# Score bursts at alternating ends of three PSUM banks, and weights through six buffers, in a fused attention and SwiGLU kernel

## The chip, the cores and the metric

The kernel runs on one core of a Trainium2 chip. The metric is the device time of one execution in microseconds (us); a lower time is better. The time before is 532.54 us, the median of three runs (531.28 to 533.48).

## What is computed

Eight batches of eight heads attend over 576 tokens with a head dimension of 64. A score survives only if it is within `tau` (0.02) of the largest of its row; the softmax runs over the survivors. The 4608 rows of 512 that come out are normalised and go through a SwiGLU layer with an inner width of 1536.

```python
scores = scale * np.matmul(q, k.transpose(0, 1, 3, 2))
thresh = np.max(scores, axis=-1, keepdims=True) - tau
scores = np.where(scores >= thresh, scores, -1000000000.0)
scores = scores - np.max(scores, axis=-1, keepdims=True)
attn = np.exp(scores)
attn = attn / (np.sum(attn, axis=-1, keepdims=True) + 1e-09)
attn_out = np.matmul(attn, v)
...
x = attn_out.transpose(0, 2, 1, 3).reshape(B * S, H * D)
xn = x / np.sqrt(np.mean(x * x, axis=-1, keepdims=True) + 1e-06) * rms_g
g = xn @ w_gate
return (g / (1.0 + np.exp(-g)) * (xn @ w_val)) @ w_out
```

## The kernel before

**Steps.** The work is cut into 144 steps. A step is one chunk of 128 query rows (`chunks`, L281) with one pair of heads; four steps make a chunk, and 36 chunks cover all rows. The first 16 steps belong to batch 0, and batch 1 begins at step 16. For each step:

- TensorE multiplies the queries with the keys of both heads (`emit_burst`, letter S) into PSUM, 576 columns per head. The matmuls are float32, on 64 rows each.
- VectorE reduces each head (`ttr`, letter r): it copies the scaled scores to SBUF (tile `ssb`) and takes the largest (tile `mx`, or `mxp` for a piece that is not the last of its head). When it has read a PSUM bank, that bank is free again.
- GpSimd (POOL) adds `tau` to get the threshold (`nthr`, letter n, tile `nth`).
- ScalarE masks each head (`prelu`, letter p, two per step) and takes the exponential of both (`ex2`, letter x, tile `wsb`).
- The weights are transposed: for the first 16 steps on TensorE, in two PSUM banks (letter T), with two copies by VectorE (letter S on VectorE, tile `wt`); later by a DMA transpose that SP issues (letter t).
- TensorE multiplies them with the values for two steps at a time (`emit_av`, letter A), and VectorE divides by the sum (letter h, tile `xsb`).

After the fourth step of a chunk the rows are squared on ScalarE (letter S there, tile `xn`), normalised on POOL (m, N) and transposed. A group of two or four chunks then goes through the feed-forward layer (`emit_ffn`, L1048): twelve gate products (G) and twelve value products (V) on TensorE, tanh on ScalarE (t), two products on VectorE (s, g; tiles `sl` and `hf`), and the output products (O).

**Bursts.** `plan_bursts` (L787) cuts the scores into TensorE bursts as the constant `CHOP` (L1302) says: kind "w" for steps 0 to 8, bursts of 1024 columns for steps 8 to 24, and bursts of 1536 columns from there on. A "w" burst is one step: each head is cut in two halves of 288 columns on the two sides of a bank border, so it fills parts of banks 0 and 1 for head 0, and 3 and 4 for head 1, the same for each step. A burst of 1024 or 1536 columns takes up to two or three banks per head and begins and ends inside a step where it has to; a step that is cut needs two reductions per head in place of one. PSUM has eight banks. Transposes and the other products take single banks, whose numbers follow the letter in the order: `T67` uses banks 6 and 7.

**Order.** `ORDER` (L43) lists the instructions of each engine, one letter for each unit of work as `LETTERS` (L26) names them. A letter takes the oldest unit of its kind that is left; `.k` after it skips k of them. `in_order` (L128) turns this into queues. Each engine works through its own queue strictly in this order, and waits where its next unit is not ready; DMAs from SP are issued in SP's order. Costs and due times in the source no longer set the order; the texts do.

**Weights.** The gate and value weights come in twelve loads of 512 KB (L1216, letter i on SP), each into one of three stages of the tile `stg` (L255), in turn. POOL scales and rounds each load in two casts (letter c; tiles `wg` and `wv`). A load waits for the casts of the load that had the stage before. The last stage also holds the first query rows at the start (L447). The 24 buffers `hf` for the hidden values are twelve of their own and twelve that lie on the stages (L257, L258); the first gate into one of the latter waits for all casts (L1100). Output weights are four loads that POOL issues (letter M).

The batch loads are D, d, m, M (batch 0's queries and keys), L and o (batch 1's queries, keys and tails), O and A (values), l and a (later batches). TensorE transposes batch 1's queries and keys in four units (letter q) and tails (k, l).

Of the kernel before, what the change touches and what calls it, by code (L numbers as in the profile page):

```python
# [10 lines left out]
FP16 = mybir.dt.float16  # L11
# [1382 lines left out]
```

## Time and profile before

| what | value |
|---|---|
| median of three runs | 532.54 us (531.28 to 533.48) |
| profiled execution, its own time | 533.18 us |
| its span, first to last instruction | 531.4 us |
| TensorE (PE) busy | 508.1 us, 96% |
| VectorE (DVE) busy | 459.5 us, 86% |
| ScalarE (ACT) busy | 443.9 us, 84% |
| GpSimd (POOL) busy | 224.0 us, 42% |
| granted TensorE clock | 0.999 |
| prelu (`ssb<-ssb,nth`) | 288 of 766 ns |
| exponential (`wsb<-ssb`) | 144 of 1157 ns |
| weight loads (`stg<-in_moe_w_gate_dram`, `stg<-in_moe_w_val_dram`) | 12 of 512 KB, 4.9 and 5.2 us from issue to landing |

The profile is of one execution. Nearly all instructions carry the line number of one helper (L99), so a group is known by its tiles: `bank<-qkt` is a score matmul, `bank<-id,wsb` a weight transpose, `bank<-xnT,wg` a gate product, `ssb<-bank,zcol` a reduction. A busy TensorE is not TensorE at its peak, because matmuls are pipelined and their ends are modelled. Waits name the engine and tile that came last before the wait ended. "SPq" is SP's queue of DMA issues.

### The profile page before, as it was taken

How to read it: one execution, taken by the hardware profiler on the slowest of the kernel's cores; microseconds unless marked ns; L12 is line 12 of the kernel's file. 1: busy time of each engine (PE TensorE's matmuls, PEld its weight loads, DVE VectorE, ACT ScalarE, POOL GpSimd, SP SyncE). 2: the span in 40 equal slices, each digit the busy share in tenths (PEclk: the TensorE clock that was granted, in tenths of full speed). 3: DMA queues.
4: the chain of work that ended last, by engine and by line, in shares of the span. 5: the costliest groups of instructions: out<-in, count | busy, mean ns of one | idle time of the engine just before them, and what ended most of it. 6: DMA issues, size and time to landing. Idle time of an engine off the chain costs nothing.

```text
span 531.4 us, 14442 instructions
## 1 busy us (share of the span) xinstructions
PE 508.1 (96%) x5344; PEld 268.0 (50%) x5344; DVE 459.5 (86%) x1276; ACT 443.9 (84%) x648; POOL 224.0 (42%) x478
## 2 busy tenths in 40 slices
PE   7887889999989999999999999999999999989995
PEld 4555655564545455545455444544545455444442
DVE  4899989998999799999998989998999898864653
ACT  5999989998799899799999889889899889971211
POOL 0464678445742446517553255726751230121000
PEclk9999999999999999999999999999999999999999
DMA  9999899799979999898989998999885686555202
GB/s 198 251 252 214 223 208 197 136 233 204 171 144 156 175 208 174 167 195 154 224 152 174 186 176 158 190 199 213 179 150 107 146 156 113 103 107 110 59 21 80
DMA packets 218887, 88.52 MB, mean 167 GB/s; under 512 B 195264, under 2 KB 204992, under 8 KB 218816
## 3 DMA queue, kind: packets, MB, share of 16 engines
q1 hardware_dynamic: 216016, 85.49, 81.2%
q0 software_dynamic: 1600, 1.57, 1.8%
q8 instruction: 42, 0.69, 0.5%
q10 hardware_dynamic: 1200, 0.52, 0.3%
q14 instruction: 29, 0.24, 0.2%
HBM read 37.75 MB, written 9.44 MB: 89 GB/s over the span
## 4 chain that ended last, share of the span: by engine, by line
PE 66%; DVE 5%; DMA 3%; ACT 2%; issue 2%; POOL 1%; SPq 0%; POOLq 0%; DVEq 0%; ACTq 0%
PE bank L99 66%; DVE ssb L99 3%; DMA wt<-wsb 2%; ACT ssb L99 1%; DVE qkt L99 1%; ACT wsb L99 1%; DMA qkx<-in_k_dram 1%; DVE hf L99 1%; DVE sl L99 1%; ACT th L99 0%; DVE xsb L99 0%; POOL spare L99 0%; POOL qkx L99 0%; DVE stg L99 0%; ACT xn L99 0%
## 5 line engine op out<-in xcount | busy, mean ns | idle before, releaser
L99 ACT ACTIVATE ssb<-ssb,nth 128x576 f32<-128x576 f32 x288 | 209.6, 766 | 14.4 <-POOL nth L99 14.1
L99 DVE CUSTOM_DVE_ANT_0 ssb<-bank,zcol 128x576 f32<-128x576 f32 (+5 forms) x288 | 182.9, 671 | 17.5 <-PE bank L99 12.7
L99 ACT ACTIVATE wsb<-ssb 128x1152 f16<-128x1152 f32 x144 | 165.6, 1157 | 2.1 <-DMA wt<-wsb 0.4
L99 PE MATMUL bank<-qkt 64*64 64x512 f32 (+11 forms) x2232 | 155.6, 410 | 5.4 <-DVE mx L99 3.9
L99 PE MATMUL bank<-xnT,wg 128*128 128x512 f16 (+1 forms) x480 | 113.3, 358 | 2.9 <-DVE mx L99 2.1
L99 PE MATMUL bank<-xnT,wv 128*128 128x512 f16 (+1 forms) x480 | 113.3, 358 | 0.3
L99 POOL TENSOR_SCALAR nth<-mx 128x2 f32<-128x2 f32 x144 | 30.8, 214 | 183.2 <-DVE mx L99 171.3
L99 PEld LDWEIGHTS bank<-qkt 64*64 64x64 f32 (+1 forms) x2232 | 73.3, 134 | 63.5 <-issue 23.6
L99 ACT ACTIVATE th<-bank 128x512 f32<-128x512 f32 (+1 forms) x120 | 64.9, 545 | 48.0 <-PE bank L99 47.3
L99 DVE SCALAR_TENSOR_TENSOR sl<-th,bank 128x512 f32<-128x512 f32 (+1 forms) x120 | 74.1, 626 | 19.3 <-ACT th L99 18.8
L99 PEld LDWEIGHTS <-wg 128*128 128x128 f16 x480 | 43.3, 98 | 56.1 <-DVE mx L99 7.3
L99 PEld LDWEIGHTS <-wv 128*128 128x128 f16 x480 | 44.6, 98 | 47.7 <-DVE mx L99 3.5
L99 PEld LDWEIGHTS <-wt 128*128 128x128 f16 (+1 forms) x1440 | 51.2, 100 | 19.4 <-issue 2.6
L99 PE MATMUL bank<-va,wt 128*128 128x65 f16 (+3 forms) x1440 | 54.9, 196 | 2.3 <-DMA wt<-wsb 1.0
L99 PE MATMUL bank<-wo,stg 128*128 128x512 f16 x216 | 51.3, 379 | 0.0
L99 PE MATMUL bank<-wo,hf 128*128 128x512 f16 x216 | 50.8, 379 | 0.0
L99 DVE STREAM_TRANSPOSE qkt<-qkx 128x128 f32<-128x128 f32 (+2 forms) x72 | 41.0, 586 | 0.4 <-POOL qkx L99 0.4
L99 DVE CUSTOM_DVE_ANT_0 ssb<-bank,zcol,mxp 128x384 f32<-128x384 f32 (+7 forms) x76 | 36.2, 508 | 3.2 <-issue 2.1
L99 DVE TENSOR_TENSOR stg<-bank,sl 128x512 f16<-128x512 f32 (+1 forms) x60 | 36.8, 628 | 2.0 <-PE bank L99 1.2
L99 DVE TENSOR_TENSOR hf<-bank,sl 128x512 f16<-128x512 f32 (+1 forms) x60 | 37.0, 628 | 0.9 <-PE bank L99 0.4
L99 POOL COPY spare<-qkx 32x576 f32<-32x576 f32 x48 | 31.6, 658 | 13.1 <-DMA qkx<-in_k_dram 7.5
L99 DVE TENSOR_TENSOR xsb<-bank,rz 128x256 f32<-128x256 f32 x72 | 30.6, 425 | 5.5 <-POOL xn L99 1.4
(45 smaller groups left out, 373.9 us busy)
## 6 DMA issues: line engine op xcount, KB each, us to landing
vst<-in_v_dram SPq DMA_DIRECT2D x32, 256.0 KB, 4.1
qkx<-in_k_dram SPq DMA_DIRECT2D x24, 288.0 KB, 3.7
qkx<-in_q_dram SPq DMA_DIRECT2D x24, 288.0 KB, 3.6
out_dram<-osb SPq DMA_DIRECT2D x48, 128.0 KB, 2.6
stg<-in_moe_w_gate_dram SPq DMA_DIRECT2D x6, 512.0 KB, 4.9
stg<-in_moe_w_val_dram SPq DMA_DIRECT2D x6, 512.0 KB, 5.2
wt<-wsb SPq DMA_TRANSPOSE x128, 3.7
out_dram<-osb SPq DMA_DIRECT2D x8, 256.0 KB, 4.1
```

The costliest lines, as they stand in the source:

```text
L99: made = got(*args, **kw)
```

## The change

Three things change.

- `CHOP` has a new kind "y" for steps 0 to 24. A burst is one step. Even steps lie at the left end of three banks per head (banks 0 and 1 for head 0, 3 and 4 for head 1: 512 columns, then 64). Odd steps lie at the right end (banks 1 and 2, and 4 and 5: 512 columns in bank 2 or 5 first, then 64 in bank 1 or 4). From step 24 bursts have 1536 columns as before.
- `stg` has six stages. All 24 hidden buffers lie on it: the first twelve on stages 3 to 5, the others on stages 0 to 2. `W_SLOTS` says which stage each load takes. The first use of a hidden buffer waits for the casts out of stages 3 to 5, or 0 to 2.
- The five orders are written anew for their first part, and are the same from some point on. In SP's order, four weight loads now stand ahead of the first load of batch 1 (the first L); before, three L stood ahead of the first weight load and the rest were mixed. The orders of all engines differ with that.

```diff
--- before.py
+++ after.py
@@ -42,40 +42,40 @@
 )
 ORDER = dict(
     PE=(
-        "wt.1:1t0t3t.1:6St6t7t2St6t5t7ST67t2ST62t7Sq25T67ST72A6SA6q72ST65T72ST67A2T65x7Sq67A5T72Sq67T25T72Sk5x6T72A5ST67A2T65ST72A6G5T72SV6G7V2G6A5S",
-        "l67V2G5V6G7A2SV7x6G2V5G7V6A2SG7V0G6V3G1O7V4A6SG6V0G3V1x4A6SO.1:6G0OV3G1A2A7OSV6G7V3G0V1A6G4V2G5V7G6SA6V0G7V3G6V1G4V2G5V7G6SV6O7A0G3OV6SO6A3",
-        "G0OV4A1G7V6A2SG6V0G3V1G4V6A7SG7V6SG7A0V6G3V1A7O6SG7V0G3V1G4V7A2A5SOO7OA5SG6V0G3V1G4V6A7SG6V0G3V1G4V6A7SG6O7V0A3OA6SG7V0A6G3V1O7OSG6V7G0A3V1",
-        "G4O6V7A2SOO7OA2SG6V0G3V1G4A6V7SG6V0G3V1G4V7A6SA6O7G0V3OA2SG6V0G7O6V3OSG6V0A3G1V4A7G2V6SO6A7OO7A2SG6V0G3V1G4A6V2OSG7V0G3V6G1A4V7SO6G0OV3A5A7S",
-        "G6V0O7A3G1OV6SG6A0V3G1V4G6V7SO6OA0O7A6SG6V0G3V1A2G4V6OSG6V0G3V1G4V6A2SO6G0A3OV2A7SG6O7V0G3OV2SG6A0V3G7V1G4A6V7SA7O6OA7SG7V0G3V1G4A6O7OSV7G6",
-        "V0G3V1G4V6A2A7SO6G7OV2SG7A0V3G1V4O7OSA6G7V0G3V6G4V7A2SA7O6OSG6V0G3A1V6G4A7V6SG6A7V0G3V1G4V6O7SOG1A2V6G0V3G2V1G0A6V7G5A6V3G0O2OA6V7O5OO1OO7O",
-        "G3V0G5V4G3O2OV0G6V5G2V3O6G4V5G7OO0134V2G6OV7G2V6OOG7OOV5OG7V5G6V7OOOOOOOOOOOOOOOOO",
+        "wt2t.1:5t7t.2:1St5t6t7St7St.1:5T67t4t3ST67SA6T67St3T67ST67ST67SA2T67ST67A0A6x7Sq67Sx3T67T01q67SA2T67G0Sk6V7SG2T67SV3T67G2Sq67V5G0T67V4A1q67S",
+        "T67SG6SV7G6SV2T67A0SG6V7SG6A7SV7A6l23x5G7SV7G0A6V3G1V6G4O7V6SO.1:6x0A3A4O.1G1SOV0G6V3G7V4G6A.1:7SA7V3G0V4G1V6A2G7SV7G6A0V3G7V4G1V2G5V6G7SO6",
+        "V7G3A7OSA6V0G3V4G6O7OSV6G0A1V3G4V7G5V6SG6V7A5A2SG6A7V0G3A7V4O6SG7V0G3V4G1A2V7A5SO.1:7O.1OA2SG6V0G3V1G4V7A6SG6V0G3V1G4V6A7SG6O7V0A3OA6SG7V0A6",
+        "G3V1O7OSG6V7G0A3V1G4O6V7A2SOO7OA2SG6V0G3V1G4A6V7SG6V0G3V1G4V7A6SA6O7G0V3OA2SG6V0G7O6V3OSG6V0A3G1V4A7G2V6SO6A7OO7A2SG6V0G3V1G4A6V2OSG7V0G3V6",
+        "G1A4V7SO6G0OV3A5A7SG6V0O7A3G1OV6SG6A0V3G1V4G6V7SO6OA0O7A6SG6V0G3V1A2G4V6OSG6V0G3V1G4V6A2SO6G0A3OV2A7SG6O7V0G3OV2SG6A0V3G7V1G4A6V7SA7O6OA7SG7",
+        "V0G3V1G4A6O7OSV7G6V0G3V1G4V6A2A7SO6G7OV2SG7A0V3G1V4O7OSA6G7V0G3V6G4V7A2SA7O6OSG6V0G3A1V6G4A7V6SG6A7V0G3V1G4V6O7SOG1A2V6G0V3G2V1G0A6V7G5A6V3",
+        "G0O2OA6V7O5OO1OO7OG3V0G5V4G3O2OV0G6V5G2V3O6G4V5G7OO0134V2G6OV7G2V6OOG7OOV5OG7V5G6V7OOOOOOOOOOOOOOOOO",
     ),
     ACT=(
-        "lT.1TT.2TT.1TTpTpxTTppxppTxppxpVppxpxpVSppxpxppxVppppxxVSppxEppxpppxpppxxpptpxpSxtpptxppvvxpttpSxptpptpxSxppttxtpppxpxppttpxpxppxtppStxppxpp",
-        "xptpttxStpptxppxSttptptptpxxpptxppxppxpptSxpptxSptptxptpppxxptpxpppxptpxtpppxxSptpxtptppxSpxppxppppxStptxtpppxxpptptxtpxppxSpptxppxpptxpStpp",
-        "pxxpptptxptSxppxppxppppSxtxtpptxppxpptptxtpxppSxpptppxppxtxtpSppxpxppxpttptxpSpxppxpppxpxSttpptxppxptpxtptpxppxptppxSpxppxtpptSxppxpptxtpptx",
-        "SppxpppxppxpxttSpptxppxptpxttppxpSppxtpppxppxxptSptpxpxppxttpptxSppxpppxpxptptxtSppxppxppxttptppxpxpptpxpppxtppStppxSxxppptxtptxSppxppppxpxt",
-        "pptxptpxSpxppttp.2p.2txppx.1xSpptxp.2tpptxpxtSttStttttttttttteses",
+        "lT.1TT.3TTTTTppxTp.1Tpxppxppxp.1pTxp.1pxp.1pxppxSp.1pxSp.1Vpxp.1pxVpptxpEpp.1txpp.1pxtpVpxtp.1pVx.1xp.1tpSxtp.1pp.1pxp.1txptxppp.1vvpxtSxp.1",
+        "pp.1ttxp.2tp.1pxxppSxpptpxSpxppttxtp.1pxppxptptxptpSxp.1pxt.1Stptpttxppxp.1tpppxxppp.1txtpSpxpxptpxp.3tp.2tp.1x.1pxpptxpppxSptxtp.1pp.1xpSx",
+        "p.1ptxp.1ttpxp.1Spxppxp.1ppxSptptxtpxppxpptptxptxppxSpptxppxpptxpStpppxxpptptxptSxppxppxppppSxtxtpptxppxpptptxtpxppSxpptppxppxtxtpSppxpxppxp",
+        "ttptxpSpxppxpppxpxSttpptxppxptpxtptpxppxptppxSpxppxtpptSxppxpptxtpptxSppxpppxppxpxttSpptxppxptpxttppxpSppxtpppxppxxptSptpxpxppxttpptxSppxppp",
+        "xpxptptxtSppxppxppxttptppxpxpptpxpppxtppStppxSxxppptxtptxSppxppppxpxtpptxptpxSpxppttp.2p.2txppx.1xSpptxp.2tpptxpxtSttStttttttttttteses",
     ),
     DVE=(
-        "zCR.1RcRrrrrRRrrSSRrrSSrrVSSrrSShrrVhrrSSSSrrSSrrSxShrrrrrhrSVSrrrSrrrVSSSrrvrrhrrSSxrrSrrSSShrrrrSSrrhSSrsrgrrrrshsgrrgrrrrhssgrrxgsrrghsgr",
-        "rtTrssgrsgrghrtrTrrrrrssggxhrrtrrrru.2rseru.2sghhueurrrgrrrsshgsggstgrrsrrhrrTrrssgTggssgsgrrrrghrrseTtgrrrtrhrseghurshgurrrrrsrgsrrgshtgrrr",
-        "rrrsTuTtgrrrrshgsgrruhrrrrrrsgTrsrsghhgrrrrerrhrrrerssggsrrhgrrrrrrssggTsrhrgrrrrrrshgeututrhrrsgrTsrgrehrrrrrsrhsTgrgstTghrurrrurrrheetrrrs",
-        "rrsggsrhrrrrrrgssggshrrgrrrrrhrsTgheturtrsrrsggrurerTrrrrrtrhrssggshTgTrrrrhrurherrrrusrtsgsggrerrrrhrsrgshsrrgrrrrrrsggtherrhrsghrrstregrrr",
-        "rTrrsgsrhgsrTgrrrrurerhuhttrrrrrsrsgusghguTrrrrrsrTgsrsghrgrrrrerhsrgherrrrsrgrTsgterrrrtrrhssggshrrgrrrrrhruthtrrrerssggTTursreurhrrrgrrrTs",
-        "suggsrhhgrrrrrrsgrrrrsgesghrrerrrrrhrsrsgsrhggrrrrrrherrrsgrsghsrrgrhrrrhrrssggsrrrrr.2r.2grhrsseghsgshsggshggeessegesgessggsgesggssgsggsgsg",
-        "eeE",
+        "zCcRRrRrr.1rRr.1rSRRSr.1rS.1SrhrS.1SrrS.1SrrSSrrSSr.1hS.1rSr.1S.1Shrhxr.1rVrxS.1SSSrVrhrSsSrrgvrsrS.1SrgrS.1SsrVrS.1SgshgVr.1rSSr.1rsrrgsrgr",
+        "hSSr.1rsgrrhsrrghxsrTrrrhgssg.1gr.1rsTt.1tgrrrrr.1rhxu.1r.1hsure.1r.1rrrer.1gssgrgTTsh.1tur.1rr.1rgrhssgrhur.1sgrrrgr.1hrrrs.1stgsgssggr.1r",
+        "r.1r.2grrstThetrrhr.1grsgr.1u.1rsuerTrrr.1rrsggr.1hrTtssggrrr.2r.2rrhhsutgrrr.1hrssggr.1rhur.1rrrr.1rsTrgsrgshhgrrrr.2rre.1herrrrssggsrrhgrr",
+        "rrrrssggTsrhrgrrrrrrshgeututrhrrsgrTsrgrehrrrrrsrhsTgrgstTghrurrrurrrheetrrrsrrsggsrhrrrrrrgssggshrrgrrrrrhrsTgheturtrsrrsggrurerTrrrrrtrhrs",
+        "sggshTgTrrrrhrurherrrrusrtsgsggrerrrrhrsrgshsrrgrrrrrrsggtherrhrsghrrstregrrrrTrrsgsrhgsrTgrrrrurerhuhttrrrrrsrsgusghguTrrrrrsrTgsrsghrgrrrr",
+        "erhsrgherrrrsrgrTsgterrrrtrrhssggshrrgrrrrrhruthtrrrerssggTTursreurhrrrgrrrTssuggsrhhgrrrrrrsgrrrrsgesghrrerrrrrhrsrsgsrhggrrrrrrherrrsgrsgh",
+        "srrgrhrrrhrrssggsrrrrr.2r.2grhrsseghsgshsggshggeessegesgessggsgesggssgsggsgsgeeE",
     ),
     POOL=(
-        "SnnnrrnrrrncnrcnccnmNcccncMnMncnMrmrnNccnncnccc.1nrncrrcnmncscNncsrsMncsnscmcssncNssnssnsssnssnsnsssssssmnNnnmnnNnmNnmNnrr.2sssnsnsr.2r.2rsn",
-        "rsnsnssssmsssnNnmNsssnsssnsnssr.1nnnr.1nmrNnnmNnnrrnmnNnrssssnssnssnsnsnsssmsssnssNnnnmsr.1nsssNsmNnsr.1nnrnnsnrsnssnrssnmssssNmnssrnnNsnr.1",
-        "ssnssssnnmsr.1sNnssmnsNnnmrnnNnnrssnsnrsnsnrsmsnNsnsnnssmsnNsmNnnssssnsssnssssr.1nmnNr.1nsnnnsnsssmrnssnrNmsrsNnssnsnrssssmsNnnsnsnr.1ssss",
-        "r.1nsnmNnnnnnrnnmrrNnnmNnrmNnnnnnmnnnnNn.1mnmNNmN",
+        "Snnr.3nr.1r.3rrnc.2nc.9nc.9nc.2c.1rr.2nc.6c.3cnmNc.2ncmNncc.5c.5ncc.3nnc.1r.1nMc.1nM.1cr.3nnrc.5c.2nmnMNsc.3nc.1r.1rcnsscnsMnsssnsnssmsNnsnn",
+        "msssssNnsssnssssnnmNnmnr.4Nr.1nnmNssr.1ssrsnnsnsssssnrsnssmsnssnnsNrssssssnn.1nmNnnnr.4mnNr.1nmnr.2NrnrnmNnnrssssnssnssnsnsnsssmsssnssNnnnms",
+        "r.1nsssNsmNnsr.1nnrnnsnrsnssnrssnmssssNmnssrnnNsnr.1ssnssssnnmsr.1sNnssmnsNnnmrnnNnnrssnsnrsnsnrsmsnNsnsnnssmsnNsmNnnssssnsssnssssr.1nmnNr.1",
+        "nsnnnsnsssmrnssnrNmsrsNnssnsnrssssmsNnnsnsnr.1ssssr.1nsnmNnnnnnrnnmrrNnnmNnrmNnnnnnmnnnnNn.1mnmNNmN",
     ),
     SP=(
-        "MmmMddDdDOOODADLLSLOiiLOiiLALLLioio.1ioOiiOillittlOlttittlltlltttAttTttattsaTtllatsaTTttllttlltttAlstlTtttTtaatattttsTattTtllstltlstAlttlttT",
-        "ttlsTlttatsattTatTtlallttAlttttlslsTtltTtslttattTtstTatsttlltaattlttlstltTtTlttstlTtlTatAtatatstsallTtttlstllltttstTlttlAtTTattstttattTtttss",
-        "aatttTtTsttTttttttstt.1ttTttTsTssTsssssss",
+        "m.1MmdMddDD.1DO.1AO.2OSi.1Di.4Oi.3iL.3Ai.1LLiLooi.2O.2O.2i.1oLiOi.2L.2L.1LOi.1llitltttlttttl.1lttllttAta.2a.1taTs.1ttasTl.1lttTTlltttltltt",
+        "l.1lt.1ttTatttssa.2ta.1tTttAatTtTttllts.1ltsltAlttlttTttlsTlttatsattTatTtlallttAlttttlslsTtltTtslttattTtstTatsttlltaattlttlstltTtTlttstlTtlT",
+        "atAtatatstsallTtttlstllltttstTlttlAtTTattstttattTtttssaatttTtTsttTttttttstt.1ttTttTsTssTsssssss",
     ),
 )
 
@@ -252,10 +252,10 @@
     NT_ = 3
     th = [sb(f"th{i}", [128, 512]) for i in range(NT_)]
     sl = [sb(f"sl{i}", [128, 512]) for i in range(NT_)]
-    stg = sb("stg", [128, NSTAGE * 1024])
-    stage = [stg[:, 1024 * i:1024 * (i + 1)].rearrange("p (e n) -> p e n", e=2) for i in range(NSTAGE)]
-    hf = [sb(f"hf{i}", [128, 512], FP16) for i in range(12)]
-    hf += [stg.bitcast(FP16)[:, 512 * i:512 * (i + 1)] for i in range(NHF - 12)]
+    stg = sb("stg", [128, 2 * NSTAGE * 1024])
+    stage = [stg[:, 1024 * i:1024 * (i + 1)].rearrange("p (e n) -> p e n", e=2) for i in range(2 * NSTAGE)]
+    hf = [stg.bitcast(FP16)[:, 512 * i:512 * (i + 1)] for i in list(range(12, 24)) + list(range(12))]
+    assert NHF == 24 and NSTAGE == 3
     osb = [sb(f"osb{i}", [128, DM]) for i in range(2)]
     osb += [ssb[i % NSB][:, i // NSB, 0:DM] for i in range(4)]
 
@@ -780,7 +780,7 @@
                 t.reads = list(banks(at[h], hi - lo))
                 t.opens = [b for b, last in last_use.items() if (last[1] == h and n_ == len(segs) - 1 if TILE else last == (n_, h))]
 
-    stage_use = []
+    stage_use, first_use = [], []
     ssb_user = {}
     last_burst = []
 
@@ -793,6 +793,14 @@
                     at = 1536 * (x % 2) if kind == "xx" else 0
                     plan.append(([(x, 0, S, (at, at + 1536 - S))], x, [
                         [(x, (0, TAIL), (MAIN, S), (at, at + 1024))], [(x, (MAIN, 0), (S, TAIL), (at + 512, at + 1024 - TAIL))]]))
+            elif kind == "y":
+                for x in range(lo, hi):
+                    if (x - lo) % 2 == 0:
+                        at, parts = 0, [(0, MAIN), (MAIN, S)]
+                    else:
+                        at, parts = 1536 - S, [(TAIL, S), (0, TAIL)]
+                    plan.append(([(x, 0, S, (at, 1536 + at))], x, [
+                        [(x, (f,) * 2, (t,) * 2, (at + f, 1536 + at + f))] for f, t in parts]))
             elif kind == "d":
                 for x in range(lo, hi, 2):
                     cut = 1024 - S
@@ -1097,7 +1105,7 @@
             t = add("ACT", n / 1.2 + 49.0, pr - PUSH[0], [g, th_use.get(i)], tanh, src=(g, 0))
             s_ = add("DVE", el, pr - push1, [t, sl_use.get(i)], silu, frees=(g, 0))
             th_use[i] = s_
-            m_ = add("DVE", el, pr - push1, [s_, vv] + (stage_use if hi >= 12 and hi not in hf_use else []), gate, frees=(vv, 0))
+            m_ = add("DVE", el, pr - push1, [s_, vv] + ([] if hi in hf_use else stage_use if hi >= 12 else first_use), gate, frees=(vv, 0))
             sl_use[i] = m_
             hs.append((hi, m_))
             uses += [g, vv]
@@ -1216,7 +1224,7 @@
     for c in range(DFF // 512):
         for d in range(0, 4, 2):
             for w_dram, w_sb in ((moe_w_gate, wg), (moe_w_val, wv)):
-                slot = n // 2 % len(stage)
+                slot = W_SLOTS[n // 2]
                 pr = W_FROM + W_STEP * n
 
                 def load(o, d=d, w_dram=w_dram, c=c, slot=slot):
@@ -1234,7 +1242,7 @@
 
                     ca = add("POOL", COST["cast_w"], pr + W_STEP * e, [lo, o_g], cast)
                     w_use[slot].append(ca)
-                    stage_use.append(ca)
+                    (first_use if slot >= NSTAGE else stage_use).append(ca)
                     w_done[c].append(ca)
                 n += 2
     wo_ld = []
@@ -1299,7 +1307,7 @@
 SQ_DVE = (0,)
 OUT_DVE = (1,)
 LAGS = ()
-CHOP = ((0, 8, 'w'), (8, 24, 1024), (24, 144, 1536))
+CHOP = ((0, 24, 'y'), (24, 144, 1536))
 LONG = 1024
 TILE = False
 TTR_EARLY = 1.0
@@ -1331,6 +1339,7 @@
 HALF_PRIO = 1.2
 WAYS = ("pp",)
 NSTAGE = 3
+W_SLOTS = (0, 1, 3, 4, 5, 2, 0, 1, 2, 0, 1, 2)
 N_W = 3
 NZ = 1
 SQ_POOL = 99
```

## The prediction

> **What bounds the kernel now.** I read the chain of work that ended last first, from its end.
>
> ```profile
> 173.34 4.91 DMA wt<-wsb
> 178.24 0.05 issue
> 178.29 282.78 PE bank L99 x3004
> 461.07 1.54 issue
> ```
>
> From 178.3 to 461.1 us the chain is TensorE alone. The texts of the five orders are the same from some point on; counting letters up to it (39 G, 39 V and 27 A on TensorE, 120 p and 59 x on ScalarE) and finding those instructions in the trace puts the point at 186 us on TensorE and 195 us on ScalarE. By then both kernels have done the same work, except for how score bursts are cut. So the time after equals the time before, less how much sooner that point is reached. Then I read the busy time by stretch (the columns are PE, PEld, DVE, ACT, POOL).
>
> ```profile
> core 0: us, PE busy (x) PEld busy (x) DVE busy (x) ACT busy (x) POOL busy (x), PEclk, DMA share, GB/s
> 0.00:10.00 10.00, 7.63 (x44) 3.96 (x44) 4.21 (x17) 3.60 (x10) 0.70 (x7) 1.00 0.91 168
> 10.00:72.00 62.00, 53.72 (x750) 36.50 (x751) 56.89 (x188) 59.82 (x89) 33.35 (x68) 1.00 0.99 236
> 72.00:80.00 8.00, 6.31 (x83) 3.75 (x82) 5.92 (x19) 6.47 (x12) 7.04 (x15) 1.00 1.04 199
> 80.00:122.00 42.00, 40.73 (x521) 24.26 (x518) 41.33 (x131) 41.20 (x66) 25.03 (x51) 1.00 0.92 185
> 122.00:146.00 24.00, 22.88 (x228) 11.91 (x227) 21.25 (x58) 18.82 (x28) 14.97 (x31) 1.00 1.05 197
> 146.00:187.00 41.00, 39.44 (x428) 19.64 (x428) 37.50 (x103) 39.31 (x57) 16.42 (x39) 1.00 0.88 160
> ```
>
> Between 10 and 72 us, where the score bursts are recut, ScalarE is busy 59.8 of 62 us and TensorE idles 8.3. From 80 us TensorE, VectorE and ScalarE are all near full; only 122 to 146 has slack on ScalarE (5.2 us). In 72 to 80 every engine but POOL has a hole. So the changed stretch is ScalarE's, and a faster score loop can win only what ScalarE waits for. The waits of 10 to 72 us (total, times, longest):
>
> ```profile
> PE bank L99 <- DVE wt L99: 2.5, 4, 0.9
> PE bank L99 <- DVE mx L99: 1.9, 6, 0.7
> ACT qkt L99 <- PE bank L99: 1.3, 2, 0.8
> ACT ssb L99 <- POOL nth L99: 0.5, 2, 0.3
> ```
>
> TensorE does wait for the reduction that empties the score banks (mx and mxp, 1.9 + 0.8 us), but ScalarE waits 1.8 us for anything.
>
> **The change part by part**, against the profiled execution: 533.18 us, of which 531.4 are the span. The median of the runs shown is 532.54, 0.6 lower; I take my sum off the median.
>
> *Start.* Before, the first burst sits behind a transpose of query rows that it doesn't need:
>
> ```profile
> 6.58 0.55 PE L99 MATMUL bank<-id,stg 128*128 128x128 f32 x3 [0.91 <-DMA stg<-in_q_dram]
> 7.06 1.20 PE L99 MATMUL bank<-qkt 64*64 64x288 f32 x16
> ```
>
> The new order has that transpose after the burst: at most 0.9 us. Against it, the key tail that the burst does need is issued third on SP, not second; the issue placed ahead takes 0.6 us. I take +0.3 (from -0.6 to +0.9).
>
> *Score bursts, steps 0 to 24.* A "w" burst fills the banks that the next one needs; a "y" burst meets the one before only in banks 1 and 4, with 64 columns. The Trainium skill ("Perfetto Trace Analysis", Optimization Strategy) says that a gap which repeats on the engine that should be saturated can mean too little PSUM. By that rule the repeated TensorE waits (2.7 us) would all come back; by the row the saturated engine is ScalarE, so the ceiling is its 2.2 us of idle time. The row decides: +1.0, half (0 to 2.2).
>
> TensorE's work hardly moves: a step as 16 half-bank matmuls takes 1.20 us, and 24 matmuls of 512, 64 and 448 columns took 1.96 us per 1024 columns, 1.10 per step. Zero, under 8.3 us of TensorE idle time; the tenth per step over 8 steps would be +-0.8 without that cover.
>
> Cutting at steps removes 16 reductions (24 pieces per head in steps 8 to 24 become 16). A whole 576-column one recurs every 0.68 us; one cut in 128 and 448 takes 0.21 + 0.61: 0.14 more. 16 x 0.14 = 2.2 us of VectorE, which ran 56.9 of 62 us there, under ScalarE's 59.8. Zero (0 to +2.2).
>
> *PSUM banks.* The bursts take banks 2 and 5 as well, so all but one of the 16 weight transposes go through banks 6 and 7 and each waits for the two copies of the last. That is the row of 2.5 us in four waits; twice it would be another 2.5 us. It hides under TensorE's 8.3 us of idle time as long as a burst is ready ahead. Zero (-2.5 to 0).
>
> *Weights.* With three stages, SP stood behind the casts:
>
> ```profile
> SPq L99 <- POOL wg L99: 15.1, 4, 9.0
> ```
>
> Its last weight load was issued at 71.5 us, and four casts (0.69 us each) ran on POOL between 73 and 80.6, between thresholds (nth) that ScalarE waits for, 1.0 us at 73.2. In the new POOL order the 24 casts end two steps earlier (ahead of the 23rd threshold, not the 25th), so about 2 x 2.7 us sooner, out of this hole. ScalarE idles 1.5 us in it and TensorE 1.7: +1.2 (0 to 1.7). POOL is also where it can go wrong: casts now stand ahead of the 5th threshold (before: the 6th), 8 of them by the 9th (before: 7), 15 by the 13th (before: 9). The second batch's loads and TensorE's transposes of them (four q) move from steps 5 to 11 to steps 11 to 17; it is first used at step 16, so nothing is late unless the loads are. The 12 hidden buffers now alias the stages; the first 12 gates wait for casts that end long before a first gate. Zero.
>
> *FFN ahead.* When step 24's burst ends, 8 G and 7 V are done instead of 5 and 4, and 8 A instead of 9; from step 37 the counts are equal. Each G or V there is four matmuls of 256 columns, 8.4 us / 56 = 0.15 each: 24 x 0.15 - 0.76 = 2.8 us of TensorE work moved into its idle time. ScalarE must follow: two tanh more (0.37 each), one prelu more (0.77), one square less (0.82): 0.7 ahead. From 80 to 122 it has no room; from 122 it has 5.2 us. So 0.7 arrives at once and up to 2.1 more later; I take +2.0 (0 to 2.8).
>
> *DMA.* The Trainium skill speaks against this part: DMAs from all issuers run on the same 16 engines and interleave ("DMA: Bandwidth & Descriptors", Issuing engines are not separate DMA queues), so twelve 512 KB loads put early slow the urgent ones. The trace agrees that there is no room: DMA share 0.99 from 10 to 72 us, and two small query issues took 8.7 us where the common one takes 3.6. By the rule alone, the batch-0 query load that is now behind the first weight would land 5 us late; by the rows it is needed at step 7, near 27 us, and issued near 15. Zero in the sum; it is the losing rival below.
>
> Sum: 0.3 + 1.0 + 1.2 + 2.0 = 4.5 us. 533.2 - 4.5 = 528.7 for the profiled run, 532.5 - 4.5 = **528.0** on the median. What is late next is ScalarE itself, from 10 us on.
>
> **The rivals.** A measurement of this kernel tells about 0.5% (2.7 us) from no change: faster is under 529.9, slower over 535.2.
>
> 1. *My forecast*: 528.0, own range 525 to 531, chance 0.48 (0.40 of it under 529.9).
> 2. *ScalarE holds everything.* The point is reached when ScalarE has done the same work; only the start and half of the score term come back, 0.8 us: 531.7. For it: 59.8 of 62 and 41.2 of 42 us. Against: the holes at 72 and 122. Chance 0.18, all but 0.03 within 0.5%. That the recut does nothing at all (bursts queued behind the transposes) ends here too.
> 3. *Casts block the thresholds: slower.* POOL works in order, and it has done this already:
>
> ```profile
> 21.59 0.21 POOL L99 TENSOR_SCALAR nth<-mx 128x2 f32<-128x2 f32 x1 [0.90 <-DVE mx L99]
> 23.71 0.69 POOL L99 TENSOR_SCALAR wg<-stg,rmsg 128x512 f16<-128x512 f32 x1 [1.91 <-DMA stg<-in_moe_w_gate_dram]
> 24.48 0.21 POOL L99 TENSOR_SCALAR nth<-mx 128x2 f32<-128x2 f32 x1
> ```
>
> The cast waited 1.9 us for its load and the threshold behind it came 0.3 us late for ScalarE. In the new order the first load leaves SP after 19 other issues, by the old times near 14.5 us, and its cast stands ahead of the threshold due at 21.5. At the 4.5 us of the old first load it lands at 19, in time; from 7 us on it is late. At 8.7 us it is 1.7 late; ScalarE has no room there, so each such stall is paid in full. Three of them, 5.1 us, with only the cast term won back: 532.5 + 5.1 - 1.2 = 536.4. Chance 0.22, 0.19 of it over 535.2.
> 4. *The holes from 122 to 187 close too*: TensorE's 1.1 + 1.6 us there and the other 1.2 us of the score term: 528.0 - 3.9 = 524.1. Against: the order is nearly the same from step 37. Chance 0.12.
>
> Faster 0.40 + 0.12 = 0.52; same 0.08 + 0.15 + 0.03 = 0.26; slower 0.03 + 0.19 = 0.22. The range runs from rival 4, less 2 us for the freed VectorE time, to just past rival 3: 522 to 537.
>
> **What would show it.** Start: no DMA wait of TensorE just before its first 64x64 burst, which starts before 7.06. Score term: ScalarE's idle time from 10 to 72 us near 1. Casts: the last weight load issued well before 71.5, and the hole of 72 to 80 filled. FFN: TensorE's idle time up to its 39th G at 12 us, not 16, and that G some 4 to 5 us before 185.6. Rival 3: thresholds that start right after a cast which waited for a weight DMA, with ScalarE waiting for nth by more than 0.5 us in all before 72 us. What would make me wrong: ScalarE starved by late loads in the first 30 us, or new holes between 80 and 186 from the rearranged transposes on SP.

## The result, and the profile after

The changed kernel takes 529.17 us (median of five, 528.46 to 530.67) against 532.37 us (531.28 to 533.48) of the kernel before beside it: a ratio of 0.9942, with a 95% interval from 0.9919 to 0.9964. Measured once more, in another set, it took 530.06 against 531.60 us, 0.9966 (0.9955 to 0.9977). By the medians the gain is 3.2 and 1.5 us; both intervals hold 0.9955 to 0.9964, a gain of 1.9 to 2.4 us. The prediction said 528.0, a gain of 4.5.

The profiled execution of the changed kernel took 530.67 us, of which 528.9 are its span: 2.5 us less than the profiled one of before on either count. The chain of work that ended last now joins TensorE for good at 116.5 us, not at 178.3 (start us, us, what):

```profile
109.84 5.04 DMA xnT<-xn
116.47 6.50 PE bank L99 x62
122.98 39.76 PE bank L99 x438
162.74 25.52 PE bank L99 x284
188.30 269.86 PE bank L99 x2843
```

From 116 us on TensorE is the path. Busy time by stretch (PE, PEld, DVE, ACT, POOL, then clock, DMA share, GB/s):

```profile
core 0: us, PE busy (x) PEld busy (x) DVE busy (x) ACT busy (x) POOL busy (x), PEclk, DMA share, GB/s
10.00:72.00 62.00, 56.42 (x785) 34.51 (x784) 56.91 (x160) 60.05 (x88) 35.55 (x72) 1.00 1.03 241
72.00:80.00 8.00, 7.90 (x124) 5.13 (x116) 6.33 (x21) 7.97 (x14) 5.62 (x11) 1.00 1.23 194
80.00:122.00 42.00, 38.68 (x504) 22.74 (x504) 39.40 (x126) 39.36 (x63) 25.44 (x52) 1.00 1.03 189
122.00:146.00 24.00, 23.99 (x245) 11.79 (x247) 23.68 (x64) 22.11 (x31) 16.43 (x32) 1.00 0.88 177
146.00:187.00 41.00, 41.00 (x482) 21.03 (x474) 37.56 (x106) 39.65 (x58) 15.09 (x36) 1.00 0.93 182
```

ScalarE's idle time, before and after: 2.18 and 1.95 us from 10 to 72, 1.53 and 0.03 to 80, 0.80 and 2.64 to 122, 5.18 and 1.89 to 146, 1.69 and 1.35 to 187. In all 11.4 us became 7.9. TensorE is full from 122 us on; up to its 39th gate product it idles 11.2 us, before 16.3. That product ends at 182.9 us, before at 185.9: 3 us sooner, not the 4 to 5 of the prediction.

Two accounts can be made of these 3 us. ScalarE idles 3.5 us less and works 0.7 more (443.9 and 444.6 us busy): 2.8. TensorE idles 5.1 us less, but its score matmuls got longer; this is their row among the costliest groups, before and after (busy us, mean ns, idle ahead of them):

```profile
L99 PE MATMUL bank<-qkt 64*64 64x512 f32 (+11 forms) x2232 | 155.6, 410 | 5.4 <-DVE mx L99 3.9
```

```profile
L99 PE MATMUL bank<-qkt 64*64 64x64 f32 (+7 forms) x2280 | 157.9, 410 | 2.7 <-ACT qkt L99 1.1
```

2.3 us more: 5.1 - 2.3 = 2.8. The wait for the reductions (mx) is gone from the row, and work has come in its place. Taking the end of each numbered exponential in both traces, the changed kernel leads by 2.8 us at the 7th, by 0.5 at the 13th, is 2.0 behind at the 19th, level at the 37th, 1.0 behind at the 41st, 3.9 ahead at the 43rd, and 2.7 to 3.0 ahead from the 61st to the end. The step from the 41st to the 43rd is a hole of before that is gone: near 137 to 140 us TensorE, VectorE and ScalarE all stood in turn, behind a weight transpose that SP had issued behind key and query loads. Of the kernel before:

```profile
137.89 0.47 PE L99 MATMUL bank<-va,wt 128*128 128x130 f16 x9 [1.00 <-DMA wt<-wsb]
138.40 0.18 DVE L99 RECIPROCAL rz<-bank 128x4 f32<-128x4 f32 x1 [1.09 <-PE bank L99]
139.08 0.63 ACT L99 ACTIVATE xn<-xsb 128x512 f16<-128x512 f32 x1 [1.67 <-DVE xsb L99]
```

From the 42nd to the 43rd exponential the kernel before takes 8.1 us, the changed one 4.2. It is the largest single step of the lead. The other runs below agree on what it goes with: 7.7 us with the old orders and six buffers (e4_six), 4.2 with the new orders, with three buffers (e5_three) and with six feed-forward products moved later (e10_ffnback). So it comes with the new orders; which of their changes closes the hole no run tells.

The start, and the waits between 10 and 72 us, of TensorE and then ScalarE (total, times, longest):

```profile
6.64 1.20 PE L99 MATMUL bank<-qkt 64*64 64x512 f32 x16 [0.33 <-ACT qkt L99]
```

```profile
PE bank L99 <- DVE wt L99: 1.5, 5, 0.5
...
ACT qkt L99 <- PE bank L99: 0.7, 2, 0.5
ACT ssb L99 <- POOL nth L99: 0.7, 2, 0.3
```

The first burst waits for no DMA and starts 0.4 us sooner, yet the first mask starts at 10.60 us, not 10.39 (10.35 in a second trace of the changed kernel). From 80 to 187 us ScalarE waits for:

```profile
ACT th L99 <- PE bank L99: 1.9, 3, 0.9
ACT ssb L99 <- POOL nth L99: 1.1, 2, 0.8
ACT xn L99 <- DMA xnT<-xn: 1.1, 1, 1.1
ACT wsb L99 <- DMA wt<-wsb: 0.9, 1, 0.9
```

The last two rows are new; they are DMA transposes, at 113.9 and 109.0 us. The first two were longer before, 3.3 and 2.5 us, and a wait of 1.7 us for `xsb` is gone. SP's waits for casts up to 80 us have shrunk from 20.9 us (15.1 for wg, 5.8 for wv) to this, and the last weight load leaves at 57.5 us, not 71.5:

```profile
SPq L99 <- POOL wv L99: 3.7, 1, 3.7
```

On POOL the danger that the prediction named is there, and just misses. A cast waits 2.7 us for its weights, and the threshold comes straight behind it:

```profile
20.82 0.69 POOL L99 TENSOR_SCALAR wv<-stg,rmsg 128x512 f16<-128x512 f32 x1 [2.73 <-DMA stg<-in_moe_w_val_dram]
21.59 0.21 POOL L99 TENSOR_SCALAR nth<-mx 128x2 f32<-128x2 f32 x1
22.88 0.69 POOL L99 TENSOR_SCALAR wv<-stg,rmsg 128x512 f16<-128x512 f32 x1 [1.07 <-DMA stg<-in_moe_w_val_dram]
```

### The profile page after: what moved, and what is told of

It reads as the page before. It is cut to its first block, busy times and chain, and to the rows that moved or that the text cites. A ratio compares the mean times of both kernels' runs of the same rounds, so it can differ in the third digit from the quotient of the medians.

```text
span 528.9 us, 14506 instructions
## 1 busy us (share of the span) xinstructions
PE 510.3 (96%) x5392; PEld 264.9 (50%) x5392; DVE 457.6 (87%) x1244; ACT 444.6 (84%) x648; POOL 224.2 (42%) x478
## 4 chain that ended last, share of the span: by engine, by line
PE 80%; DVE 10%; ACT 3%; DMA 2%; issue 2%; SPq 1%; POOL 0%; DVEq 0%; ACTq 0%; POOLq 0%
PE bank L99 80%; DVE ssb L99 5%; ACT ssb L99 2%; SPq L99 1%; DMA stg<-in_moe_w_val_dram 1%; DVE qkt L99 1%; ACT wsb L99 1%; DVE stg L99 1%; DVE sl L99 1%; DMA xnT<-xn 1%; DVE xsb L99 1%; DVE wt L99 0%; ACT qkt L99 0%; DVE rz L99 0%; DVE osb L99 0%
## 5 line engine op out<-in xcount | busy, mean ns | idle before, releaser
L99 ACT ACTIVATE ssb<-ssb,nth 128x576 f32<-128x576 f32 x288 | 209.9, 766 | 11.9 <-POOL nth L99 11.4
L99 DVE CUSTOM_DVE_ANT_0 ssb<-bank,zcol 128x576 f32<-128x576 f32 (+2 forms) x288 | 188.8, 687 | 16.5 <-PE bank L99 11.5
L99 PE MATMUL bank<-qkt 64*64 64x64 f32 (+7 forms) x2280 | 157.9, 410 | 2.7 <-ACT qkt L99 1.1
L99 PEld LDWEIGHTS bank<-qkt 64*64 64x64 f32 x2280 | 71.9, 133 | 71.4 <-issue 24.4
L99 PE MATMUL bank<-wo,stg 128*128 128x512 f16 x432 | 101.6, 379 | 0.0
L99 DVE TENSOR_TENSOR stg<-bank,sl 128x512 f16<-128x512 f32 (+1 forms) x120 | 73.7, 628 | 3.1 <-PE bank L99 1.9
L99 PEld LDWEIGHTS <-stg 128*128 128x128 f16 x432 | 40.6, 98 | 54.4 <-DVE stg L99 3.6
L99 POOL COPY spare<-qkx 32x576 f32<-32x576 f32 x48 | 31.6, 659 | 11.2 <-DMA qkx<-in_k_dram 7.5
L99 POOL COPY qkx<-spare 32x576 f32<-32x576 f32 x48 | 31.7, 660 | 3.0
L99 POOL COPY qkx<-qkx 32x576 f32<-32x576 f32 x48 | 31.6, 658 | 3.0
```

The costliest lines, as they stand in the source:

```text
L99: made = got(*args, **kw)
```

## The experiments

My theory: the gain comes from earlier loads and casts and from feed-forward work that fills holes, and the alternating bursts make room for that order. Rivals: the bursts themselves bring it; the six buffers bring it; TensorE's work or ScalarE's work alone decides up to the point where the orders become the same. Leads and delays below are taken at the same numbered exponential of two profiled executions, against the first trace of the changed kernel where no other is named; times are medians. Runs of different sets ran on different chips, so each is given as a ratio to the kernel before beside it as well. The diffs below show only the lines that matter, and of the orders one or two engines.

### Score bursts

**All bursts at the left end (e1_left).** Products between bursts that used banks 0, 1, 3 and 4 go through 2 and 5, so they have fewer banks as well.

```diff
-                    if (x - lo) % 2 == 0:
+                    if True:
```

> The changed kernel, but every burst of steps 0 to 24 lies at the left end (banks 0, 1 and 3, 4), so a burst meets all banks of the one before; transposes and products that used banks 0, 1, 3 or 4 between these bursts take 2 and 5. Pieces of 512 and 64 columns, weights and the rest of the orders stay. ScalarE theory (it is the bound up to 72 us, a later burst hides): within 1 us of the changed kernel, 529.2 to 530.2, with TensorE's waits for mx and mxp before 72 us back at 2.5 us or more. Rival (the alternating ends are the gain): most of the 3.2 us is lost, 531.5 or more.

544.81 us, 1.0244 (1.0226 to 1.0262) of before: 15.6 us over the changed kernel's 529.17. ScalarE is busy 50.2 of the 62 us from 10 to 72, and TensorE waits there for the reductions:

```profile
PE bank L99 <- DVE mx L99: 12.5, 14, 1.4
```

The delay grows step by step, 2.0 us at the 7th exponential, 9.8 at the 17th, 14.3 at the 23rd, and stays at 14.4 to the end. The rival's "531.5 or more" holds, and by far: in the new order the alternating ends, with the banks that they leave to other products, carry 15 us. But the kernel before, with its own order, paid for the same conflict with 2.7 us of TensorE waits only, and ScalarE's idle time there fell by only 0.2 us with the change.

**The recut alone (e3_y8).** The kernel before, with "y" bursts in steps 0 to 8 and its own orders.

```diff
-CHOP = ((0, 8, 'w'), (8, 24, 1024), (24, 144, 1536))
+CHOP = ((0, 8, 'y'), (8, 24, 1024), (24, 144, 1536))
```

> The kernel before, with the alternating bursts for steps 0 to 8 in place of the halves; weights and all orders as before. ScalarE theory: no more than 0.5 us of gain, 532.0 to 532.6. Rival (the alternating ends are the gain): a third of 3.2 us or more, 531.3 or less. TensorE's busy time in score matmuls: the same as before within 0.3 us if a step in 512 and 64 columns costs what two halves cost, so that the changed kernel's extra 2.3 us come from steps 8 to 24.

546.12 us, 1.0269 (1.0251 to 1.0287). Neither expectation had this. The old order puts transposes of keys, queries and weights in banks 2 and 5, which these bursts need; TensorE waits 5.8 us for reductions (mx, mxp) and 8.0 us for copies of transposed keys and queries (qkt) between 10 and 72 us, and ScalarE for thresholds:

```profile
ACT ssb L99 <- POOL nth L99: 11.6, 5, 3.6
```

Against the trace of before, 12.8 us are lost by the 7th exponential, 16.7 by the 11th. The granted clock fell to 0.81 in that stretch, and some bursts took 2.20 us instead of 1.20. So the run says nothing of what the bursts cost TensorE, and how much of the loss is the conflict over banks and how much the clock is open. What stands is that the recut of the first 8 steps does not fit the old order, as the new order does not work without the alternation.

### Weights

**Six buffers alone (e4_six).** The changed source, with the bursts and all five orders of before.

```diff
-CHOP = ((0, 24, 'y'), (24, 144, 1536))
+CHOP = ((0, 8, 'w'), (8, 24, 1024), (24, 144, 1536))
```

> The kernel before with the six weight buffers and the hidden buffers laid over them; bursts and all orders as before, so weight loads keep their places in SP's order and casts theirs in POOL's. Theory (the order brings the gain, the buffers only allow it): SP's waits for the casts, 21 us, mostly vanish and the last weight load is issued by 60 us, but the casts stay in their places, ScalarE's hole from 72 to 80 us stays, and the time is 531.9 to 532.9. Rival (the buffers are the gain): 530.5 or less.

531.63 us, 0.9999 (0.9989 to 1.0009): nothing, as expected. But SP's waits did not vanish. It still waits for casts, 13.0 us for wv and 3.3 for wg, and the last weight load leaves at 71.7 us: it is the place of the loads and casts in the queues that makes it wait, more than a lack of buffers.

**Three buffers with the new order (e5_three, e5b_three), and the changed kernel beside it (a0_after).** Loads and casts stand at the same places of SP's and POOL's queues, in their natural order.

```diff
-W_SLOTS = (0, 1, 3, 4, 5, 2, 0, 1, 2, 0, 1, 2)
+W_SLOTS = (0, 1, 2, 0, 1, 2, 0, 1, 2, 0, 1, 2)
```

> The changed kernel with only stages 0 to 2 in use for the weights, in turn, loads and casts in their plain order at the same places in the queues. Theory (the weights' early loads are needed for the early casts and for the FFN's head start): SP stands behind casts again for 15 us or more, casts and thresholds behind them wait, 531.5 to 534. Rival (the bursts are the gain): 529.2 to 530.0.

First 530.58 us (530.04 to 532.27), 0.9978 (0.9967 to 0.9989), a smaller loss than expected. The changed kernel had not run beside it, so both were then run side by side.

> The changed kernel as it is, beside the others of this set. Both theories: 0.994 of the kernel before, 528.5 to 530.5 us. It is the yardstick for the two kernels that follow.

> The changed kernel with three stages for the weights in place of six, loads and casts in their natural order at the same places of the queues; measured again, this time beside the changed kernel itself. Theory A (the order of the loads does it, the three added buffers only make it safe): within 0.5 us of the changed kernel. Theory B (six buffers are needed for the early loads): 1 to 1.5 us slower than the changed kernel, which is what the first run of it would give against the first times of the changed kernel (530.6 against 529.2).

The changed kernel took 530.06 us (528.93 to 530.54), the one with three buffers 531.25 (529.11 to 536.57), a ratio to before of 1.0001 (0.9978 to 1.0023). In this set the kernel with three buffers has no gain left in the median; it is 1.2 us behind the changed kernel. The best executions are alike; it is the spread that differs, 1.6 us in 7 executions against 7.5 in 12 (2.2 us in the 12 of the first set). The profiled execution, 534.46 us, shows one of the long ones. TensorE reaches the transposes of batch 1's queries at 52.8 us and waits:

```profile
PE bank L99 <- DMA qkx<-in_q_dram: 2.9, 1, 2.9
```

With three buffers SP stands 8.0 us behind casts (wg 5.1, wv 2.9), and what comes behind leaves later; the issue of the last query load ahead of that wait ran from 45.84 us:

```profile
45.84 4.49 SPq L99 DMA_DIRECT2D qkx<-in_q_dram  x1
```

In the changed kernel beside it SP waited 3.6 us, and the load in that place of the queue was through at 45.8:

```profile
42.08 3.69 SPq L99 DMA_DIRECT2D qkx<-in_q_dram  x1
```

From the 13th to the 21st exponential 4.3 us are lost against the changed kernel beside it, and 4.4 stand at the end. The wait is 2.9 of them; behind it the granted clock fell to half:

```profile
57.10:60.60 3.50, 3.50 (x42) 3.16 (x43) 2.39 (x8) 3.06 (x5) 0.21 (x1) 0.51 0.87 196
```

In the first profiled execution (530.04 us) SP stood behind casts as long, 8.1 us, but the same issue ended at 48.2, not 50.3, and TensorE did not wait. So the new order can gain with three buffers, and I read the six as what keeps its loads from coming late now and then; that rests on one long execution and on one of two sets. Theory A holds for the best executions, theory B for the median of the second set: neither as I had put it.

**Four loads of batch 1 ahead of the first weight load (e6_Lfirst).** In SP's order:

```diff
-OSi.1Di.4Oi.3iL.3Ai.1LLiLooi
+OSL.3LLLi.1Di.4Oi.3iAi.1iooi
```

> The changed kernel with the first four loads of batch 1 issued ahead of the first weight load; all else the same. Theory (weights must be ahead of the second batch, or the early casts hold the thresholds): ScalarE's waits for nth before 72 us grow from 0.7 to over 3 us and most of the gain is lost, 531 to 534. Rival (ScalarE has enough queued, loads are hidden either way): 529.2 to 530.0.

534.71 us, 1.0050 (1.0035 to 1.0066): 4.7 us slower than the changed kernel of the second set. This is what the prediction's third rival feared:

```profile
23.78 0.69 POOL L99 TENSOR_SCALAR wv<-stg,rmsg 128x512 f16<-128x512 f32 x1 [6.11 <-DMA stg<-in_moe_w_val_dram]
24.55 0.21 POOL L99 TENSOR_SCALAR nth<-mx 128x2 f32<-128x2 f32 x1
```

ScalarE stands 3.7 us at 21.1, waiting for that threshold. But two more things happen at the same time. TensorE waits as long for a query load that stands behind the moved ones, and then the granted clock falls to half from 26.1 to 29.5 us, so the next burst takes 2.20 us:

```profile
24.67 0.52 PE L99 MATMUL bank<-id,qkx 128*128 128x128 f32 x3 [3.18 <-DMA qkx<-in_q_dram]
26.65 2.20 PE L99 MATMUL bank<-qkt 64*64 64x512 f32 x16 [0.97 <-ACT qkt L99]
```

ScalarE is 3.0 us late against the changed kernel at the 5th exponential, 4.0 at the 9th, 4.5 at the end. Nothing of it is won back in 500 us. The run shows what late loads cost here; it does not tell the cast's share from that of the query load.

### Feed-forward, start, and the holes after 100 us

**Three gate and three value products later (e10_ffnback).** On TensorE (ScalarE and VectorE to match):

```diff
-SG6SV7G6SV2T67A0SG6V7SG6A7SV7A6l23x5G7
+SG6SST67A0SSA7SA6l23x5V7G6V2G6V7G6V7G7SV7
```

> The changed kernel without the FFN's head start at step 24: three gate and three value products on TensorE (with their three tanh on ScalarE and six products on VectorE) stand after the burst of step 23, so that 5 G and 4 V are done when it ends, as in the kernel before. Theory (the head start is the largest term, 2.0 us): 530.7 to 531.7. Rival (ScalarE decides, the head start is absorbed): 529.2 to 529.8.

536.45 us, 1.0086 (1.0067 to 1.0105), well past what I expected. The delayed products run one after another, almost all through banks 6 and 7, and ScalarE waits 1.2, 1.2 and 1.7 us between four tanh from 75.5 to 80.7. That measures a queue of my making, not the worth of the head start, which stays without a run of its own.

**Second burst ahead (e9_start).** On TensorE, and the first two masks ahead of two copies on ScalarE:

```diff
-t6t7St
+t6St7t
```

> The changed kernel with the second burst ahead of the transposes of the third pair's keys on TensorE, and the first two masks ahead of the two copies of those keys on ScalarE. Theory (before 72 us each saved us of ScalarE's waiting reaches the end): the first mask starts at 10.1 instead of 10.6 us and the time is 0.3 to 0.5 us lower, 528.7 to 528.9. Rival (a later hole, at 109 to 122 us, takes it up): 529.2.

530.62 us, 0.9975 (0.9965 to 0.9985): no gain that can be seen. Its profiled execution began badly for another reason, see the last section, so the start stays unsettled within about 1 us.

**Transposes ahead of value loads and stores near 105 us (e11_sp).** In SP's order:

```diff
-a.2a.1taTs.1ttasTl
+a.2a.1tTttaTas.1sl
```

> The changed kernel with two transposes of weights (t14, t15) and one of normalised rows (T1) moved in SP's order ahead of two value loads and two output stores, all near 100 to 110 us. ScalarE's new idle times at 109.0 (0.94 us, for a weight transpose) and 113.9 (1.09 us, for a row transpose) are what the move aims at. Theory A (the queue of issues makes these transposes late, and ScalarE's time there is carried to the end): the two idle times shrink by at least 1.2 us together, and the time falls by 1 to 2 us against the changed kernel, 527.5 to 528.5. Theory B (TensorE is what is settled near step 41, and ScalarE's idle time at 109 to 122 is cover): the idle times shrink and the time stays within 0.5 us. Theory C (the value loads are urgent): TensorE or POOL waits for the values, and the time rises by 0.5 to 2 us.

529.58 us against 530.06 of the changed kernel beside it; both ratios have the same interval within 0.0003 (0.9955 to 0.9980 here), so it is theory B by the median. In its trace ScalarE's two waits for transposes there fell from 2.2 us (beside it) to 0.8, and the delay against the changed kernel's trace falls from 1.0 us at the 33rd exponential to 0.2 at the 41st. The profiled execution had lost 1.4 us at its very start, so a gain of up to 0.8 is not excluded. But the fall of the delay does not show one: e9_start, which lacks this edit and was also late from the start, has the same fall there, from 1.9 us at the 33rd to 0.9 at the 43rd. It is the fastest median of its set, by less than can be told.

### Which engine is at its limit

**More TensorE work in steps 8 to 23 (e12_pe), more ScalarE work there (e13_act).** The first multiplies the 64-column part of each burst three times, with the same scores; the second adds an exponential of 64 columns into a tile that nobody reads.

```diff
-                    for rows, bb, lhs in quads if no_whole or o.quad else whole:
+                    again = 3 if hi[0] - lo[0] == TAIL and 8 <= s < 24 else 1
+                    for rows, bb, lhs in (quads if no_whole or o.quad else whole) * again:
```

```diff
+            if 8 <= s < 24:
+                nc.scalar.activation(out=scr, in_=sb_[:, 0, 0:64], func=AF.Exp)
             nc.scalar.activation(out=wsb[s % NW], in_=sb_, func=AF.Exp)
```

> The changed kernel with more TensorE work in steps 8 to 23: the 64-column part of each burst is multiplied three times instead of once, with the same result. By the changed kernel's trace that part adds 0.11 us to a burst (1.20 us with it, 1.09 without), so 2 x 16 x 0.11 = 3.5 us more TensorE work before 75 us; the bursts of the change themselves added 2.3 us there. Theory A (what is settled near step 41 is TensorE's work, so every us of it before counts): 2.5 to 3.5 us slower than the changed kernel (530.06 beside it in the last set), 532.5 to 533.5. Theory B (ScalarE sets the pace of these steps, and TensorE's work lies in its idle time, as the prediction's zero for it says): within 1 us, 530 to 531.

> The changed kernel with more ScalarE work in the same steps 8 to 23: one more exponential, of 64 columns into a tile that nobody reads, ahead of each exponential, about 0.2 us each, 3.2 us in all. Theory A (TensorE's work is settled, ScalarE's idle time of 7.9 us from 10 to 187 us takes the rest up): 0 to 1.5 us slower than the changed kernel, 530 to 531.5. Theory B (ScalarE sets the pace, paid in full): 3 us or more, 533 and above. If this and the run with more TensorE work are both paid in full, both engines are at their limit there, and neither term of the sum could have been put at zero.

With more TensorE work: 533.55 us, 1.0033 (1.0020 to 1.0047) of before, where the changed kernel has 0.9966 (0.9955 to 0.9977) in the set before: 3.5 us slower. The score row of its page:

```profile
L99 PE MATMUL bank<-qkt 64*64 64x512 f32 (+8 forms) x2512 | 162.6, 393 | 2.4 <-ACT qkt L99 0.7
```

The row is 4.7 us longer than the changed kernel's; a part of it overlaps other matmuls, and TensorE's busy time in all grew by 3.1 us (510.7 to 513.8). Its idle time up to 187 us was 10.4, against 10.2 in the second trace of the changed kernel (a0_after). Not a tenth of the work went into that idle time. The delay against that trace is there by the 27th exponential, 3.2 us, and stays. ScalarE feels it: from 10 to 72 us it is busy 58.2 us, not 60.5.

With more ScalarE work: 531.07 us, 0.9984 (0.9975 to 0.9993), 1.0 us slower. The added row is the first below, but ScalarE's busy time grew by 1.9 us only (444.5 to 446.4), not by 16 x 0.25 = 4.0, for in the trace 13 of them start about 0.1 us before their predecessor ends, and each time the next instruction starts about 0.1 us before they end themselves:

```profile
L99 ACT ACTIVATE scr<-ssb x16: 242/251/269, 33.5 to 80.6; 128x64 f16<-128x64 f32 x16
```

Of 1.9 us, ScalarE's idle time up to 187 us took up 1.1 (13.7 to 12.6), and 0.7 to 1.0 were paid. So TensorE's added work counts in full in these steps, ScalarE's about by half. Both times fall where theory A put them, and the prediction's view that the changed stretch belongs to ScalarE alone does not hold. Two things stay open. The added matmuls lengthen the very bursts that reductions, thresholds and masks wait for, so it can be that path, and not TensorE's pace as such, that was paid for; no run adds TensorE work elsewhere. And the two runs have the changed kernel of another set as their measure.

## Why the prediction was right, and where its sum was not

It was right in sign and in a part of its mechanism: faster, settled by the point from which the orders are the same, with the holes of 72 to 80 and 122 to 146 filled. It was wrong on which engine the first 72 us belong to. Of the 4.5 us, 2.5 to 2.9 came in the profiled executions, and 1.9 to 2.4 by the two sets of times together: about half, which the range of 525 to 531 was wide enough to hold. Term by term:

- **TensorE's work of the bursts, 0 (+-0.8): the step that failed.** The text said that a step of 1.20 us instead of 1.10 would hide "under 8.3 us of TensorE idle time". It also counted that tenth over 8 steps, but the steps that went from 1.10 to 1.20 are the 16 from 8 to 24: 1.6 us by its own figures. The row grew by 2.3 us. And the idle time was no cover: e12_pe added 3.1 us of the same work in the same steps and paid 3.5. TensorE's idle time there is many waits of its own, each for an operand or a bank and none longer than 0.8 us in the changed kernel; I read it as work between them moving them all back, beside the path through each burst that e12_pe leaves open.
- **Score bursts, +1.0: 0.2.** ScalarE idles 1.95 instead of 2.18 us from 10 to 72. ScalarE waited for anything 1.8 us in all before, as the text itself read; taking half of its 2.2 us of idle time was a guess, and the wait that went (mx, from 1.9 to 0.2 us for TensorE) made way for work. e1_left shows that without alternation the new order costs 15 us, which is a cost avoided, not a gain on before.
- **Start, +0.3: about 0.** The first burst starts 0.4 us sooner and the first mask 0.2 us later (0.04 sooner in the second trace).
- **Casts and the hole of 72 to 80, +1.2: 1.5** in that window. e4_six shows that six buffers alone do not bring it, and the first run of e5_three that the new orders can with three (ScalarE idles 0.05 us in that window).
- **Feed-forward ahead, +2.0: at most 1.8**, not measured by itself. ScalarE's idle time from 122 to 187 us fell by 3.6 (TensorE's by 2.7), but 1.8 came back as new holes from 80 to 122, the "new holes between 80 and 186 from the rearranged transposes on SP" that the text gave as a way to be wrong. Two of the three are DMA transposes behind loads. The 3.6 need not be the head start's at all: the largest piece, the hole ahead of the 43rd exponential, is just as closed in e10_ffnback, which moves six of the products back behind the burst of step 23.
- **Reductions and banks, 0: right.** VectorE worked 1.9 us less in all (2.2 forecast), and the waits for weight copies (wt) did not double but fell from 2.5 to 1.5 us.
- **DMA, 0: right, narrowly.** The first weight load left at 13.9 us (14.5 forecast) and took 6.75 us, between the 4.5 and 8.7 that were weighed. A cast waited for it by 2.7 us, and ScalarE's waits for thresholds came to 0.7 us up to 72, above the mark of 0.5, but no stall of the size of rival 3 came. e6_Lfirst shows that such a stall is not won back: with a TensorE wait for a query load at the same time and 3.4 us at half clock behind them, it cost 4.5 to 5 us. The rival's 5.1 us came near that by other terms (three stalls of 1.7). What kept it away was that four weight loads stand ahead of the first loads of batch 1 in SP's order.

With TensorE's work at its measured 2.3 in place of 0, the sum is 2.2 us, 530.3, against 529.2 and 530.1 measured. This agreement was found afterwards and is not a proof. The errors of the other terms are left out of it: they are ScalarE's account, which comes to 2.8 us by itself (3.5 less idle, 0.7 more work), and I read the longer bursts as already in it, in what the score term lacks and in the new holes. How much of each is theirs no run shows.

## What to carry to other kernels

Idle time that is made of many short waits for operands is no safe cover for added work: here it took up 0.2 us of 3.1, while another engine was busier. A run with a little duplicated work measures that. When each engine works in a fixed order, a delay of some microseconds early on can reach the end almost whole (4.5 us in e6_Lfirst, 14.4 in e1_left; of the 1.8 in e9_start 1.0 was left), so margins of the first loads are worth more than an average of busy time shows. A wider buffer can change little in the best executions and still matter in the long ones.

## What the runs showed of the hardware

**The first bursts can run at half speed.** The same burst of 16 matmuls took 1.20 us in the changed kernel's executions, and in the profiled ones of e9_start and e11_sp this (here e11_sp):

```profile
7.07 2.20 PE L99 MATMUL bank<-qkt 64*64 64x512 f32 x16
```

The granted clock of that stretch is given as 1.00 all the same, but that is no reading: in these two traces the record of the clock begins only at 10.3 us (at 4.3 to 6.0 in the others), and a stretch without a record counts as 1.00. By the next burst the matmuls were at their usual time. Both executions had a delay of 1.4 to 1.8 us at the first exponential against the changed kernel's trace. The Trainium skill ("TensorE: Matmul & The Clock Gate", The HAM clock gate) has the first matmuls at half rate for a time that varies from run to run; that agrees with 2.20 against 1.20. As 1.0 us of such a delay was still there at the end of e9_start, and 0.1 in e11_sp, it can make a part of the 1 to 2 us by which executions of one kernel differ, which is as much as half of the whole effect here or more.

**The clock can fall to half where TensorE waits.** Three traces show the granted clock at half within the first 72 us, and with it bursts of 2.20 us in place of 1.20 in two of them: e6_Lfirst for 3.4 us, 1.4 us after the end of a wait of 3.18 us; e5b_three for 3.4 us, 1.4 us after the end of a wait of 2.91; and e3_y8 three times, for 6.8, 10.2 and 6.8 us, near waits of 1.74, 2.95 and 1.71. In the first two a late load was paid twice, with the wait and with slower matmuls behind it. Neither the longest wait nor the idle share alone tells when: e10_ffnback waited 1.81 us at a stretch with the clock at 1.00, and from 10 to 72 us e1_left, busy for 44.6 of 62 us, stayed at 1.00, where e3_y8, busy for 46.5, had 0.81.
